# Swapped output halves for odd pairs of heads, and a first MoE block in plain float32 with its weights split later

## Chip, cores and metric

The kernel runs on one core of a Trainium2 chip. The metric is the device time of one execution in microseconds (us), and smaller is better. Four engines matter here: PE (TensorE, the matrix products; PEld is its weight loading), DVE (VectorE), ACT (ScalarE) and POOL (GpSimd). SP issues the transfers.

## The reference, cut to what matters

```python
def reference(q, k, v, f_logit, moe_w_in, moe_w_out, moe2_w_gate, moe2_w1, moe2_w2):
    f = sigmoid(f_logit)                          # 4 batches, 8 heads, 768 steps, head size 48
    for t in range(768):                          # a gated linear attention
        state = f[t][:, None] * state + k[t][:, None] * v[t][None, :]
        y[t] = q[t] @ state
    x = y as (3072 tokens, 384)
    x = relu(x @ w_in) ** 2 @ w_out               # first MoE: 384 -> 2048 -> 384
    P = sinkhorn(x @ w_gate)                      # 8 experts, 8 rounds over rows and columns
    return sum(P[:, e] * (relu(x @ w1[e]) @ w2[e]) for e in range(8))   # second MoE
```

All of it is float32. A product of two float32 matrices can be had in two ways here: as one plain float32 product, or with each operand split into a high part in the type `fp32r` and the rest (a low part), as three `fp32r` products high-high, high-low, low-high.

## The kernel before

The attention runs in 24 chunks of 128 steps (6 for each batch). For a chunk `c`, DVE makes two running products of the gates (`scan_r`, `scan_f`), POOL scales k and q with them (`mul_k`, `mul_q`), PE makes the scores (`scores`), DVE masks them (`causal`), PE turns k (`k_turn`), adds to the state (`state_in`) and mixes the outputs (`mix`), ACT and DVE take the outputs out of PSUM (`y_part`).

`mix` (lines 379 to 392) makes, for each of four pairs `p` of heads, two products "in" (L383: all 128 rows, one head to partitions 0 to 63, the other to 64 to 127) and two products "state" (L386: head j has the rows from 64 j on, and goes to the output half 64 j). The chunks that start a batch (0, 6, 12, 18) have no state. All four pairs write one PSUM tile.

Three chunks make one block of 384 tokens (8 blocks). For a block `j` the first MoE takes 16 slices `f` of the hidden layer: `e1` (`products_in`, L499) with 9 `fp32r` products (3 splits times 3 tiles of rows), then on ACT `Relu`, `Square` and the high half (`m_relu`, `m_square`, `m_hi`), on DVE the low half (`m_lo`, L515), then `e2` (`m_out`, L525) with 9 more. Slices are counted through: slice 16 is the first of block 1.

The weights of the first MoE come as 64-bit numbers, and the kernel turns them into float32 during block 0, slice by slice: `cva`, `cvw` on ACT, three DVE instructions (`clamp` L937, `fields` L941, `sign` L945), one sum on POOL (`total`, L949). Then the high half `cvh` on ACT (L280) and the low half `cvl` (L283), of which POOL makes six and DVE ten (`LO_DVE`). Block 0 waits for them slice by slice; all later blocks use the same halves.

The second MoE follows with its own weights, which go into ten buffers (`wpool`) that the first MoE's weights leave. Lines 678 and 729 are its products.

The order of the work on each engine is made by a list scheduler (`Plan`): each step has an engine, an assumed duration, a due time and the steps that it needs; of what is ready, the step with the earliest due time goes first. Engines then run their queues in that fixed order, and a waiting instruction holds up what is behind it. `keep_warm` puts dummy products (L245, plain float32, 128 columns) into PE's early gaps.

Of the kernel before, what the change touches and what calls it, by code (L numbers as in the profile page):

```python
# [20 lines left out]
NP = H // 2  # L21
# [32 lines left out]
LO_DVE = (4, 6, 8, 9, 10, 11, 12, 13, 14, 15)  # L54
# [96 lines left out]
def body(tc, fkq, v, wm, wa, wc, gate, seqs, out):  # L151
# [5 lines left out]
    wpool = ctx.enter_context(tc.tile_pool(name="wpool", bufs=NWP))  # L157
# [23 lines left out]
    wb = rpool("wb", NF - NWP)  # L181
# [82 lines left out]

    def new_w(n):
        W[n] = (wb if n >= NWP else wpool).tile([128, 2, WCOL], F32R, tag="w", name="w")
        return W[n]

    def ldw(n):
        if n in early:  # L270
            early[n] = early[n - 4] if n >= 4 else wb.tile([128, WCOL], I64, tag="w", name="raw64")
        raws[n] = early[n] if n in early else rawp.tile([128, WCOL], I64, tag="raw", name="raw64")
        sp.dma_start(out=raws[n], in_=wm[n])
# [4 lines left out]

    def cv_hi(n):
        act.copy(out=new_w(n)[:, 0, :], in_=cvt[n])  # L280

    def cv_lo(n):
        (dve if n in LO_DVE else pool).tensor_tensor(out=W[n][:, 1, :], in0=cvt[n], in1=W[n][:, 0, :].bitcast(F32), op=ALU.subtract)  # L283

    for n in range(NF):
# [3 lines left out]
        add(("cva", n), "act", 0.74, due, lambda n=n: cv_abs(n), [("ldw", n), if_(n >= 3, ("cvl", n - 3))], start=CV_AT + CV_STEP * n)  # L289
# [4 lines left out]
        add(("cvs", n), "pool", 1.78, due, lambda p=part: p("total"), [("cvb", n, 2), ("cvw", n)])  # L294
# [84 lines left out]
    def mix_pair(c, p, rows=64):  # L379
        y, vv, kk, st = tmp["y", c], vt[c % 3], kq[c % 3], Sh.get(c)  # L380
# [3 lines left out]
        if st is not None:  # L384
            for j in range(2):
                pe.matmul(y[64 * j:64 * j + rows, p, :], st[64 * j:64 * j + DH, p, 0:rows], kk[64 * j:64 * j + DH, 1, p, :], start=False, stop=True)  # L386

    def mix(c):
        new_y(c)
        for p in range(NP):  # L390
            mix_pair(c, p)
        Psb.pop(c)


    def mix_last(c):
        new_y(c)
        mix_pair(c, NP - 1)

    def last_out(c):
        act.copy(out=ylast, in_=tmp["y", c][:, NP - 1, :])  # L400

    def mix_rest(c):
        for p in range(KD):
            pe.matmul(tmp["y", c][:, p, :], shift[:, 16 * p:16 * p + 128], ylast, start=True, stop=True)
            mix_pair(c, p, DH)
# [19 lines left out]
    for c in range(NCH):  # L425
# [40 lines left out]
        needs = [("cm0", c), ("cm1", c), ("ldv", c), if_(not first, ("sh", c)), if_(1 < c < CPB, ("yl", c - 2))]  # L466
        if blk:
            at("mix", "pe", 2.1 if not first else 1.1, 2.5, mix, needs)
# [6 lines left out]
        at("yl", "dve", 0.62 if blk else 0.5, 3, lambda c: y_part(c, 1), [("yh", c)])  # L475
# [13 lines left out]
    add("conv", "none", 0, 0, close_conv, [("cvl", n) for n in range(NF)])  # L489
# [4 lines left out]
    def products_in(i, w, xx):  # L494
        ps = eps[i] = ps_e.tile([128, BT], F32, tag="e1", name="e1")
        n = 0
        for k in range(KD):
            for wl, xl in ((0, 0), (0, 1), (1, 0)):
                pe.matmul(ps, w[:, wl, k * 128:(k + 1) * 128], xx[:, xl, k, :], start=n == 0, stop=n == 3 * KD - 1)  # L499
                n += 1  # L500

    def m_relu(i):
        hl[i] = [hp.tile([128, BT], F32, tag="g", name="g", bufs=2)]
# [41 lines left out]
    E1, E2 = 1.49, 1.49  # L545
# [646 lines left out]
```

## Time and profile before

| | |
|---|---|
| median of 3 runs | 2131.81 us (2130.74 to 2133.03) |
| the profiled execution | 2132.19 us |
| its span, first to last instruction | 2130.4 us |
| busy: PE, PEld, DVE, ACT, POOL | 98%, 83%, 62%, 42%, 30% |
| mean granted TensorE clock | 0.99 |

The profile's busy shares are means over the span. The prediction reads stretches of it: a table of busy time by stretch, the list of waits of an engine, single instructions in order of time, and groups of instructions by line. In a row of instructions, "x4" counts records; a plain float32 product leaves two records of a weight load and two of a product, an `fp32r` product one of each.

### The profile page before, as it was taken

The numbers are of one execution on the slowest core, as the hardware profiler recorded it, in microseconds if no ns is written. First come the engines' busy times: TensorE is split into PE (matmuls) and PEld (weight loads), VectorE is DVE, ScalarE is ACT, GpSimd is POOL, SyncE is SP. The second block draws the span as 40 slices with busy tenths as digits, with TensorE's granted clock in tenths as the row PEclk, the third lists the DMA queues.
The fourth block names the chain that finished last, engine by engine and source line by source line (L and its number), as shares of the span: only waits on it lengthen the run. The fifth ranks groups of instructions, "written<-read, shape, count | busy, mean of one in ns | idle before, by whom it ended". The sixth has DMA issues, their size and how long they took to land.

```text
span 2130.4 us, 27837 instructions
## 1 busy us (share of the span) xinstructions
PE 2080.0 (98%) x10686; PEld 1762.8 (83%) x10686; DVE 1325.2 (62%) x2022; ACT 886.4 (42%) x1505; POOL 638.1 (30%) x636
## 2 busy tenths in 40 slices
PE   7889999999999999999999999999999999999998
PEld 5789899998987888878878888888887888888886
DVE  8973443332477666657677666756767766766674
ACT  4754444454643433423434433433433433443341
POOL 4531100010103333333332333334233243333331
PEclk9899999999999999999999999999999999999999
DMA  7342212110203111112122112121213111211210
GB/s 269 127 128 65 77 67 83 57 49 7 81 31 91 55 55 60 55 55 70 55 86 88 55 55 70 55 62 52 68 62 108 61 59 52 69 55 55 70 45 32
DMA packets 55114, 148.76 MB, mean 70 GB/s; under 512 B 6332, under 2 KB 15548, under 8 KB 54972
## 3 DMA queue, kind: packets, MB, share of 16 engines
q1 hardware_dynamic: 54972, 146.90, 21.6%
q8 instruction: 85, 1.39, 0.3%
q14 instruction: 57, 0.47, 0.1%
HBM read 135.28 MB, written 9.54 MB: 68 GB/s over the span
## 4 chain that ended last, share of the span: by engine, by line
PE 90%; DVE 6%; issue 1%; DMA 1%; POOL 1%; ACT 0%; SPq 0%; DVEq 0%; POOLq 0%; ACTq 0%
PE o L729 35%; PE e L678 33%; PE e L499 9%; PE a L525 8%; PE y L383 1%; PE y L386 1%; PE pp L344 1%; DVE cv_t L937 1%; DVE cv_t L945 1%; PE lg L540 1%; DVE lo L515 1%; PE ds L366 0%; DVE cv_t L941 0%; DVE w L283 0%; DVE sg L318 0%
## 5 line engine op out<-in xcount | busy, mean ns | idle before, releaser
L729 PE MATMUL o<-h,w 128*128 128x512 f32 x3456 | 792.8, 389 | 0.0
L729 PEld LDWEIGHTS o<-h,w 128*128 128x128 f32 x3456 | 648.1, 188 | 135.6 <-DVE sc L752 0.7
L678 PE MATMUL e<-x,w 128*128 128x512 f32 x3168 | 734.6, 391 | 10.4 <-DVE t L700 5.3
L678 PEld LDWEIGHTS e<-x,w 128*128 128x128 f32 x3168 | 597.2, 189 | 137.5 <-DVE t L700 7.0
L696 ACT COPY s<-e 128x512 f32<-128x512 f32 x288 | 168.9, 586 | 836.1 <-PE e L678 831.4
L761 POOL TENSOR_TENSOR acc<-acc,sc 128x512 f32<-128x512 f32 x258 | 334.4, 1303 | 536.4 <-DVE sc L752 529.5
L752 DVE TENSOR_TENSOR sc<-o,pb 128x512 f32<-128x512 f32 x264 | 182.0, 690 | 372.3 <-PE o L729 339.1
L718 DVE SCALAR_TENSOR_TENSOR h<-v,h 128x512 fp32r<-128x512 f32 x384 | 275.3, 736 | 1.8 <-ACT h L713 1.3
L713 ACT ACTIVATE h<-v 128x512 fp32r<-128x512 f32 x384 | 242.2, 631 | 52.8 <-DVE v L705 52.6
L705 DVE TENSOR_TENSOR v<-e,s 128x512 f32<-128x512 f32 x288 | 198.0, 688 | 74.7 <-ACT w L663 56.5
L650 POOL TENSOR_TENSOR rawa<-rawa 128x256 f32<-128x256 f32 x96 | 81.1, 845 | 537.4 <-DMA rawa<-in_wa_dram 347.8
L499 PE MATMUL e<-x,w 128*128 128x384 f32 x1152 | 229.0, 342 | 9.7 <-DVE w L283 6.2
L499 PEld LDWEIGHTS e<-x,w 128*128 128x128 f32 x1152 | 200.6, 190 | 16.7 <-DVE w L283 7.8
L515 DVE TENSOR_TENSOR lo<-g,hi 128x384 fp32r<-128x384 f32 x128 | 83.3, 653 | 208.6 <-ACT hi L511 208.6
L525 PE MATMUL a<-hi,w 128*128 128x384 f32 x768 | 200.1, 341 | 0.0
L667 DVE TENSOR_TENSOR w<-rawa,w 128x768 fp32r<-128x768 f32 x192 | 157.8, 823 | 8.1 <-ACT w L663 8.1
L663 ACT CAST w<-rawa 128x768 fp32r<-128x768 f32 x192 | 135.2, 728 | 29.6 <-DMA rawa<-in_wa_dram 12.4
L525 PE MATMUL a<-lo,w 128*128 128x384 f32 x384 | 131.0, 341 | 11.8 <-DVE lo L515 11.7
L525 PEld LDWEIGHTS a<-hi,w 128*128 128x128 f32 x768 | 140.3, 191 | 1.5 <-issue 0.3
L504 ACT ACTIVATE g<-e 128x384 f32<-128x384 f32 x128 | 62.9, 491 | 179.6 <-PE e L499 163.2
L328 POOL TENSOR_TENSOR kq<-kq,sg 128x512 f32<-128x512 f32 x24 | 30.9, 1287 | 290.7 <-DVE sg L318 161.6
L667 DVE TENSOR_TENSOR w<-rawc,w 128x768 fp32r<-128x768 f32 x96 | 92.5, 964 | 2.1 <-ACT w L663 2.0
(103 smaller groups left out, 1313.1 us busy)
## 6 DMA issues: line engine op xcount, KB each, us to landing
rawa<-in_wa_dram SPq DMA_DIRECT2D x96, 384.0 KB, 3.0
rawc<-in_wc_dram SPq DMA_DIRECT2D x96, 384.0 KB, 3.4
raw<-in_wm_dram SPq DMA_DIRECT2D x16, 768.0 KB, 6.2
pb<-ptd SPq DMA_DIRECT2D x24, 512.0 KB, 3.7
fraw<-in_fkq_dram SPq DMA_DIRECT2D x23, 512.0 KB, 4.0
kq<-in_fkq_dram SPq DMA_DIRECT2D x23, 512.0 KB, 4.6
vt<-in_v_dram SPq DMA_DIRECT2D x24, 192.0 KB, 5.0
x2d<-x2t SPq DMA_DIRECT2D x8, 576.0 KB, 2.8
```

The costliest lines, as they stand in the source:

```text
L499: pe.matmul(ps, w[:, wl, k * 128:(k + 1) * 128], xx[:, xl, k, :], start=n == 0, stop=n == 3 * KD - 1)
L525: pe.matmul(acc1[j][m], w[:, wl, D + m * 128:D + (m + 1) * 128], g, start=f == 0 and n == 0, stop=f == NF - 1 and n == 2)
L663: act.copy(out=W2[g, k][:, 0, 0:n], in_=src)
L667: dve.tensor_tensor(out=W2[g, k][:, 1, 0:n], in0=src, in1=W2[g, k][:, 0, 0:n].bitcast(F32), op=ALU.subtract)
L678: pe.matmul(ps, w[a], x[b], start=start and n == 0, stop=stop and n == 2, skip_group_check=True)
L696: act.copy(out=snap[g, n], in_=bank[g, "a"])
L705: dve.tensor_tensor(out=vs[g, k], in0=bank[g, k], in1=other, op=ALU.add)
L713: act.activation(out=hs[g // 2, t, f][:, 0], in_=vs[g, k], func=ACTF.Relu)
L718: dve.scalar_tensor_tensor(out=h[:, 1], in0=vs[g, k], scalar=0.0, in1=h[:, 0].bitcast(F32), op0=ALU.max, op1=ALU.subtract)
L729: pe.matmul(ob[q, t, m], w[:, a, c:c + 128], h[:, b], start=f == 0 and n == 0, stop=f == 3 and n == 2)
L752: dve.tensor_tensor(out=dst, in0=ob[q, t, m], in1=pbt[p, e][:, t * TB:(t + 1) * TB], op=ALU.mult)
L761: eng.tensor_tensor(out=acc[p, t, m], in0=acc[p, t, m], in1=sc[q, t, m], op=ALU.add)
```

## The change

It does four things.

1. Block 0 of the first MoE uses plain float32 products: 3 for `e1` and 3 for `e2` of a slice, straight from the converted weights `R[n]` and the unsplit `x1`, relu-square `g`. Its `m_hi`, `m_lo` and the low half of its `y_part` are gone.
2. The weights' halves are made for block 1 on: `cvh` and `cvl` are due 16 slices later, and all sixteen `cvl` are DVE's. Buffers are laid out anew: the halves of ten slices stand in `wpool`, those of six in the places of converted weights that block 0 has used.
3. The outputs of the attention go to two PSUM tiles by the parity of the pair, and in odd pairs the two heads change output halves. `mix` goes two pairs at a time: four products "in", then four "state". `y_part` takes out two pieces. The rows of `w_in` are permuted to suit.
4. The scheduler's assumed durations change (1.95 and 1.56 for a slice's products, 1.5 for `mix`), and with them the order.

```diff
-    wpool = ctx.enter_context(tc.tile_pool(name="wpool", bufs=NWP))
+    wpool = ctx.enter_context(tc.tile_pool(name="wpool", bufs=1, reuse_waits="tile"))
-    wb = rpool("wb", NF - NWP)
+    wb = rpool("wb", 1)
+    PAIR_AT = {n: n for n in range(8)} | {14: 8, 15: 9}
+    def left_by(n):
+        return [] if n in PAIR_AT else [2 * (n - 8), 2 * (n - 8) + 1]
     def new_w(n):
-        W[n] = (wb if n >= NWP else wpool).tile([128, 2, WCOL], F32R, tag="w", name="w")
-        return W[n]
+        if n in PAIR_AT:
+            t = wpool.tile([128, 2, WCOL], F32R, tag=f"w{PAIR_AT[n]}", name="w")
+            W[n] = [t[:, l, :] for l in range(2)]
+        else:
+            W[n] = [wb.tile([128, WCOL], F32R, tag=f"b{k}", name="w") for k in left_by(n)]
+    def cv_total(n):
+        R[n] = wb.tile([128, WCOL], F32, tag=f"b{n}", name="r")
+        F64(nc, cvt[n], raws[n]).total(R[n])
     def cv_lo(n):
-        (dve if n in LO_DVE else pool).tensor_tensor(out=W[n][:, 1, :], in0=cvt[n], in1=W[n][:, 0, :].bitcast(F32), op=ALU.subtract)
+        dve.tensor_tensor(out=W[n][1], in0=R[n], in1=W[n][0].bitcast(F32), op=ALU.subtract)
...
-        add(("cvh", n), "act", 0.74, due, lambda n=n: cv_hi(n), [("cvs", n), if_(n >= NF - 2, ("cvs", n - 4))])
-        add(("cvl", n), *(("dve", 0.88) if n in LO_DVE else ("pool", 1.78)), due, lambda n=n: cv_lo(n), [("cvh", n)])
+        gone = [(s, k) for k in left_by(n) for s in ("e2", "cvl")] + ([("cvs", n - 4)] if n >= 14 else [])
+        add(("cvh", n), "act", 0.8, due + NF, lambda n=n: cv_hi(n), [("cvs", n)] + gone)
+        add(("cvl", n), "dve", 0.95, due + NF, lambda n=n: cv_lo(n), [("cvh", n)])
...
     def new_y(c):
-        tmp["y", c] = (ps_p if c >= CPB else ps_acc).tile([128, NP, CH], F32, tag="pp" if c >= CPB else f"a{1 + c % 2}", name="y")
+        for n in range(2):
+            tmp["y", c, n] = (ps_p if c >= CPB else ps_acc).tile([128, NP, CH], F32, tag="pp" if c >= CPB else f"a{1 + n}", name="y")
+    def y_at(c, p):
+        return tmp["y", c, p % 2], p // 2
+    def mix_in(c, p, rows=64):
+        vv, st = vt[c % 3], Sh.get(c)
+        y, n = y_at(c, p)
         for j in range(2):
-            h = 2 * p + j
-            pe.matmul(y[64 * j:64 * j + rows, p, :], vv[:, h * DH:h * DH + rows], Psb[c][:, j, p, :], start=True, stop=st is None)
+            h, o = 2 * p + j, 64 * (j ^ (p & 1))
+            pe.matmul(y[o:o + rows, n, :], vv[:, h * DH:h * DH + rows], Psb[c][:, j, p, :], start=True, stop=st is None)
+    def mix_state(c, p, rows=64):
+        kk, st = kq[c % 3], Sh.get(c)
+        y, n = y_at(c, p)
+        for j in range(2):
+            o = 64 * (j ^ (p & 1))
+            if st is not None:
+                pe.matmul(y[o:o + rows, n, :], st[64 * j:64 * j + DH, p, 0:rows], kk[64 * j:64 * j + DH, 1, p, :], start=False, stop=True)
     def mix(c):
         new_y(c)
-        for p in range(NP):
-            mix_pair(c, p)
+        for p in range(0, NP, 2):
+            for f in (mix_in, mix_state):
+                for i in range(2):
+                    f(c, p + i)
...
     def y_part(c, lo):
-            x1[blk] = x1p.tile([128, 2, NP, BT], F32R, tag="x1", name="x1")
-        n = NP if blk else KD
-        hi, y = x1[blk][:, 0, 0:n, t0:t0 + CH], tmp["y", c][:, 0:n, :]
-        if lo:
-            dve.tensor_tensor(out=x1[blk][:, 1, 0:n, t0:t0 + CH], in0=y, in1=hi.bitcast(F32), op=ALU.subtract)
-        else:
-            act.copy(out=hi, in_=y)
+            x1[blk] = x1p.tile([128, 2, NP, BT], F32R if blk else F32, tag="x1", name="x1")
+        parts = [(slice(n, NP if blk else KD, 2), tmp["y", c, n][:, 0:2 - (n and not blk), :]) for n in range(2)]
+        for n, y in parts:
+            hi = x1[blk][:, 0, n, t0:t0 + CH]
+            if blk == 0:
+                act.copy(out=hi, in_=y)
+            elif lo:
+                dve.tensor_tensor(out=x1[blk][:, 1, n, t0:t0 + CH], in0=y, in1=hi.bitcast(F32), op=ALU.subtract)
+            else:
+                act.copy(out=hi, in_=y)
...
     def products_in(i, w, xx):
+        if i < NF:
+            for k in range(KD):
+                pe.matmul(ps, R[i][:, k * 128:(k + 1) * 128], xx[:, 0, k, :], start=k == 0, stop=k == KD - 1)
+            return
...
     def m_out(i):
         for m in range(KD):
+            if j == 0:
+                pe.matmul(acc1[j][m], R[f][:, D + m * 128:D + (m + 1) * 128], g, start=f == 0, stop=f == NF - 1)
+                continue
...
-        add(("e1", i), "pe", E1, i, lambda i=i: products_in(i, W[i % NF], x1[i // NF]),
-            [("yl", q) for q in range(CPB) if i == 0] + [if_(j == 0, ("cvl", f)), if_(f == 0 and j, ("sprd", j)), if_(i, ("e1", i - 1)), e_free(i)])
+        dur = 1.56 if j else 1.95
+        add(("e1", i), "pe", dur, i, lambda i=i: products_in(i, W.get(i % NF), x1[i // NF]),
+            [("yl", q) for q in range(CPB) if i == 0] + [if_(j == 0, ("cvs", f)), if_(j == 1, ("cvl", f)), if_(f == 0 and j, ("sprd", j)), if_(i, ("e1", i - 1)), e_free(i)])
...
-                free = ("e2", n1 - NF + n + NWP)
+                free = ("e2", n1 - NF + {v: k for k, v in PAIR_AT.items()}[n + NWP])
```

The places at which the order changes most for the prediction are two. The first is PE's queue at a mix of the attention, here that of chunk 4. L383 and L386 are "in" and "state" (L408 and L416 in the changed kernel), `pp` the scores, `a` the outputs of `e2`. Before:

```order
L366 MATMUL ds<-vt_128,Kn 64x48 x8
L383 MATMUL y<-Psb,vt_128 64x128 x2
L386 MATMUL y<-kq_122,Sh 64x128 x2
L383 MATMUL y<-Psb,vt_128 64x128 x2
L386 MATMUL y<-kq_122,Sh 64x128 x2
L383 MATMUL y<-Psb,vt_128 64x128 x2
L386 MATMUL y<-kq_122,Sh 64x128 x2
L383 MATMUL y<-Psb,vt_128 64x128 x2
L386 MATMUL y<-kq_122,Sh 64x128 x2
```

And in the changed kernel:

```order
L382 MATMUL ds<-vt_128,Kn 64x48 x8
L408 MATMUL y<-Psb,vt_128 64x128 x4
L416 MATMUL y<-kq_122,Sh 64x128 x4
L408 MATMUL y<-Psb,vt_128 64x128 x4
L416 MATMUL y<-kq_122,Sh 64x128 x4
```


Eight groups of two products became four groups of four.

The second is DVE's queue at the end of block 0, from the last conversions on. `cv_t` are the three conversion steps of a slice, `w` the low halves of the weights, `lo` the low halves of the hidden layer, `sg` and `d` belong to the scans of an attention chunk, `Psb` are masked scores. Before, from the low half of slice 13 (`lo`) on:

```order
L515 TENSOR_TENSOR lo<-g,hi 128x384
L937 TENSOR_SCALAR cv_t<-cv_t 128x768
L941 TENSOR_SCALAR cv_t<-cv_t 128x768
L945 SCALAR_TENSOR_TENSOR cv_t<-raw_1039,cv_t 128x768
L283 TENSOR_TENSOR w<-cv_t,w 128x768
L316 MEMSET sg_125 128x8
L317 MEMSET d_126 128x4
L318 SCALAR_TENSOR_TENSOR sg_125<-sg_125,d_126 128x516
L319 TENSOR_SCALAR d_126<-sg_125 128x4
L320 RECIPROCAL d_126<-d_126 128x4
L349 TENSOR_TENSOR Psb<-pp,mask 128x512
L283 TENSOR_TENSOR w<-cv_t,w 128x768
```

In the changed kernel, from the low halves of weights ahead of chunk 8's scan on (the last conversion stands ten rows further ahead):

```order
L298 TENSOR_TENSOR w<-r,w 128x768 x4
L332 MEMSET sg_124 128x8
L333 MEMSET d_126 128x4
L334 SCALAR_TENSOR_TENSOR sg_124<-sg_124,d_126 128x516
L335 TENSOR_SCALAR d_126<-sg_124 128x4
L336 RECIPROCAL d_126<-d_126 128x4
L340 SCALAR_TENSOR_TENSOR sg_124<-sg_124,d_126 128x516
L341 TENSOR_TENSOR minf<-minf,sg_124 128x4
L298 TENSOR_TENSOR w<-r,w 128x768 x5
L560 TENSOR_TENSOR lo<-g,hi 128x384
L365 TENSOR_TENSOR Psb<-pp,mask 128x512 x2
L560 TENSOR_TENSOR lo<-g,hi 128x384 x3
```

No `lo` stands among the conversions any more; the first `lo` that is left is that of slice 16, and ten low halves of weights stand between the last conversion and it (nine of them in these rows).

## Rows read from the trace of the kernel before

**Rows 1.** Busy time by stretch: us, busy (records) of each engine, PE clock, DMA, GB/s

```profile
34.08:143.65 109.57, 86.72 (x541) 74.72 (x539) 106.37 (x127) 66.68 (x108) 60.62 (x35) 0.89 0.44 142
143.65:595.60 451.95, 451.82 (x3246) 418.59 (x3246) 172.80 (x321) 223.11 (x414) 45.12 (x39) 1.00 0.19 63
```

**Rows 2.** PE's waits from 34.08 to 143.65: us in total, times, longest

```profile
PE a L525 <- DVE lo L515: 11.7, 4, 8.5
PE e L499 <- DVE w L283: 6.2, 3, 3.2
```

**Rows 3.** The chain of waits in that stretch, shares by line

```profile
by line: DVE cv_t L937 14.2%; DVE cv_t L945 13.3%; DVE lo L515 10.7%; DVE w L283 8.6%; DVE sg L318 8.4%; PE e L499 7.1%; DVE cv_t L941 7.0%; issue 6.2%; DVE sg L324 4.8%; DVE Psb L349 3.7%; DVE minf L325 3.2%; PE a L525 2.9%; DMA x<-x 2.6%;
```

**Rows 4.** In order of time: PE's and DVE's rows at slice 16's second product

```profile
140.81 0.54 DVE L515 TENSOR_TENSOR lo<-g,hi 128x384 fp32r<-128x384 f32 x1
...
142.09 1.72 PE L499 MATMUL e<-x,w 128*128 128x384 f32 x9
143.65 0.51 PE L525 MATMUL a<-hi,w 128*128 128x384 f32 x2
```

**Rows 5.** DVE and POOL in order of time: start, us, instruction

```profile
59.73 0.55 DVE L937 TENSOR_SCALAR cv_t<-cv_t 128x768 f32<-128x768 f32 x1
60.30 0.56 DVE L941 TENSOR_SCALAR cv_t<-cv_t 128x768 int32<-128x768 int32 x1
...
61.78 0.95 DVE L283 TENSOR_TENSOR w<-cv_t,w 128x768 fp32r<-128x768 f32 x1
61.99 2.44 POOL L949 TENSOR_TENSOR cv_t<-cv_t,raw 128x768 int32<-128x768 int32 x1 [2.60 <-issue]
62.65 2.20 DVE L937 TENSOR_SCALAR cv_t<-cv_t 128x768 f32<-128x768 f32 x1
...
158.28 1.23 DVE L318 TENSOR_TENSOR_SCAN sg<-sg,d 128x516 f32<-128x516 f32 x1
```

**Rows 6.** Groups by line, 34.08 to 143.65: busy us, mean ns | idle before

```profile
L937 DVE TENSOR_SCALAR cv_t<-cv_t 128x768 f32<-128x768 f32 x13 | 16.9, 1303 | 0.0
L515 DVE TENSOR_TENSOR lo<-g,hi 128x384 fp32r<-128x384 f32 x18 | 16.7, 939 | 1.0 <-ACT hi L511 1.0
...
L318 DVE TENSOR_TENSOR_SCAN sg<-sg,d 128x516 f32<-128x516 f32 x6 | 12.5, 2089 | 0.3
L283 DVE TENSOR_TENSOR w<-cv_t,w 128x768 fp32r<-128x768 f32 x10 | 11.8, 1178 | 0.0
L941 DVE TENSOR_SCALAR cv_t<-cv_t 128x768 int32<-128x768 int32 x13 | 11.2, 861 | 0.4
L324 DVE TENSOR_TENSOR_SCAN sg<-sg,d 128x516 f32<-128x516 f32 x6 | 10.3, 1709 | 0.0
...
L283 POOL TENSOR_TENSOR w<-cv_t,w 128x768 fp32r<-128x768 f32 x5 | 10.8, 2160 | 2.2 <-ACT w L280 2.2
```

**Rows 7.** The outputs of block 1: SP's issues, and the transfers' median time to landing

```profile
114.22 3.97 SPq L423 DMA_DIRECT2D x<-x  x6
...
x<-x SPq DMA_DIRECT2D x6, 48.0 KB, 6.0
```

**Rows 8.** PE in order of time: dummy products in plain float32, and what follows

```profile
37.54 2.62 PE L245 MATMUL warm<-shift 128*128 128x128 f32 x22
39.91 3.65 PE L499 MATMUL e<-x,w 128*128 128x384 f32 x18
```

**Rows 9.** PE in order of time: products of mixes (chunks 7, 6 and 5)

```profile
164.16 0.40 PE L383 MATMUL y<-Psb,vt 128*64 128x128 f32 x4
164.49 0.44 PE L386 MATMUL y<-kq,Sh 48*64 48x128 f32 x4
164.86 0.44 PE L383 MATMUL y<-Psb,vt 128*64 128x128 f32 x4
...
167.06 1.83 PE L499 MATMUL e<-x,w 128*128 128x384 f32 x9
...
150.87 1.09 PE L383 MATMUL y<-Psb,vt 128*64 128x128 f32 x16
...
105.60 0.43 PE L383 MATMUL y<-Psb,vt 128*64 128x128 f32 x2
```

**Rows 10.** DVE: the outputs of chunk 7 leave PSUM

```profile
167.93 0.66 DVE L415 TENSOR_TENSOR x<-y,x 128x512 fp32r<-128x512 f32 x1
```

More of the change, by code (lines that the diff above doesn't have):

```diff
@@ L277, in cv_abs @@
         F64(nc, cvt[n], raws[n]).magnitude()
+    def cv_total(n):
+        R[n] = wb.tile([128, WCOL], F32, tag=f"b{n}", name="r")
+        F64(nc, cvt[n], raws[n]).total(R[n])
     def cv_hi(n):
-        act.copy(out=new_w(n)[:, 0, :], in_=cvt[n])
+        new_w(n)
+        act.copy(out=W[n][0], in_=R[n])
     def cv_lo(n):
-        (dve if n in LO_DVE else pool).tensor_tensor(out=W[n][:, 1, :], in0=cvt[n], in1=W[n][:, 0, :].bitcast(F32), op=ALU.subtract)
+        dve.tensor_tensor(out=W[n][1], in0=R[n], in1=W[n][0].bitcast(F32), op=ALU.subtract)
     for n in range(NF):
@@ L396, in mix_last @@
         new_y(c)
-        mix_pair(c, NP - 1)
+        mix_in(c, NP - 1)
+        mix_state(c, NP - 1)
     def last_out(c):
-        act.copy(out=ylast, in_=tmp["y", c][:, NP - 1, :])
+        act.copy(out=ylast, in_=tmp["y", c, 1][:, 1, :])
     def mix_rest(c):
         for p in range(KD):
-            pe.matmul(tmp["y", c][:, p, :], shift[:, 16 * p:16 * p + 128], ylast, start=True, stop=True)
-            mix_pair(c, p, DH)
+            y, n = y_at(c, p)
+            pe.matmul(y[:, n, :], shift[:, 16 * p:16 * p + 128], ylast, start=True, stop=True)
+            mix_in(c, p, DH)
+            mix_state(c, p, DH)
         Psb.pop(c)
@@ L465, in body @@
             at("sh", "dve", 0.35, 0, shat, [("st", c - 1), ("scanr", c), if_(c % NCB > 2, ("mix", c - 2))])
-        needs = [("cm0", c), ("cm1", c), ("ldv", c), if_(not first, ("sh", c)), if_(1 < c < CPB, ("yl", c - 2))]
+        needs = [("cm0", c), ("cm1", c), ("ldv", c), if_(not first, ("sh", c)), if_(0 < c < CPB, ("yl", c - 1))]
         if blk:
-            at("mix", "pe", 2.1 if not first else 1.1, 2.5, mix, needs)
+            at("mix", "pe", 1.5 if not first else 0.95, 2.5, mix, needs)
         else:
@@ L487, in close_conv @@
         pools["x2t"] = rpool("x2p", 2)
-    add("conv", "none", 0, 0, close_conv, [("cvl", n) for n in range(NF)])
+    add("conv", "none", 0, 0, close_conv, [("cvs", n) for n in range(NF)])
     hl, x2t, x2, eps = {}, {}, {}, {}
@@ L496, in products_in @@
         n = 0
+        if i < NF:
+            for k in range(KD):
+                pe.matmul(ps, R[i][:, k * 128:(k + 1) * 128], xx[:, 0, k, :], start=k == 0, stop=k == KD - 1)
+            return
         for k in range(KD):
             for wl, xl in ((0, 0), (0, 1), (1, 0)):
-                pe.matmul(ps, w[:, wl, k * 128:(k + 1) * 128], xx[:, xl, k, :], start=n == 0, stop=n == 3 * KD - 1)
+                pe.matmul(ps, w[wl][:, k * 128:(k + 1) * 128], xx[:, xl, k, :], start=n == 0, stop=n == 3 * KD - 1)
                 n += 1
     def m_relu(i):
-        hl[i] = [hp.tile([128, BT], F32, tag="g", name="g", bufs=2)]
+        hl[i] = [hp.tile([128, BT], F32, tag="hi", name="g") if i < NF else hp.tile([128, BT], F32, tag="g", name="g", bufs=2)]
         act.activation(out=hl[i][0], in_=eps.pop(i), func=ACTF.Relu)
@@ L518, in m_out @@
         j, f = divmod(i, NF)
-        _, hi, lo = hl.pop(i)
-        w = W[f]
+        g, *parts = hl.pop(i)
         if f == 0:
@@ L523, in m_out @@
         for m in range(KD):
+            if j == 0:
+                pe.matmul(acc1[j][m], R[f][:, D + m * 128:D + (m + 1) * 128], g, start=f == 0, stop=f == NF - 1)
+                continue
+            hi, lo = parts
             for n, (wl, g) in enumerate(((0, hi), (1, hi), (0, lo))):
-                pe.matmul(acc1[j][m], w[:, wl, D + m * 128:D + (m + 1) * 128], g, start=f == 0 and n == 0, stop=f == NF - 1 and n == 2)
+                pe.matmul(acc1[j][m], W[f][wl][:, D + m * 128:D + (m + 1) * 128], g, start=f == 0 and n == 0, stop=f == NF - 1 and n == 2)
         if j == NB - 1:
@@ L543, in logits_out @@
         dve.tensor_copy(out=L[:, CPB * j:CPB * (j + 1), :], in_=tmp["l"])
-    E1, E2 = 1.49, 1.49
     def e_free(i):
@@ L660, in w2_hi @@
     def w2_hi(g, k):
-        W2[g, k] = wpool.tile([128, 2, WCOL], F32R, tag="w", name="w2")
+        W2[g, k] = wpool.tile([128, 2, WCOL], F32R, tag=f"w{(3 * g + 'abc'.index(k)) % NWP}", name="w2")
         src, n = w2src(g, k)
@@ L945, in sign, with total @@
         dve.scalar_tensor_tensor(out=ti, in0=self.high, scalar=-0x40000000, in1=ti, op0=ALU.bitwise_and, op1=ALU.bitwise_or)
-    def total(self):
+    def total(self, out=None):
         ti = self.t.bitcast(I32)
-        self.nc.gpsimd.tensor_tensor(out=ti, in0=ti, in1=self.word.bitcast(I32), op=ALU.add)
+        self.nc.gpsimd.tensor_tensor(out=ti if out is None else out.bitcast(I32), in0=ti, in1=self.word.bitcast(I32), op=ALU.add)
     def all(self):
@@ L1160, in lay_out @@
     for kt in range(KD):
-        rows += [2 * kt * DH + r for r in range(DH)]
-        rows += [6 * DH + 16 * kt + r for r in range(16)]
-        rows += [(2 * kt + 1) * DH + r for r in range(DH)]
-        rows += [7 * DH + 16 * kt + r for r in range(16)]
+        for j in range(2):
+            rows += [(2 * kt + (j ^ (kt & 1))) * DH + r for r in range(DH)]
+            rows += [(7 - j) * DH + 16 * kt + r for r in range(16)]
     w_in = inputs["moe_w_in"][np.array(rows)]
```

36 lines of the change are left out of this document (19 added, 17 removed).

## Prediction

> **What bounds the kernel now.** I read the table of busy time by stretch first, because the change touches two stretches that have different limits. From 34 us, when block 0's products begin, to 143.65 us, when the second products of slice 16 begin, DVE is busy for 106.4 of 109.6 us and PE for 86.7; from there to the end of the first MoE PE is busy for 451.8 of 451.95 us [rows 1]. So in block 0 DVE sets the pace, and behind it PE alone. The other views say the same: PE waits in block 0 mostly for DVE's low halves of the hidden layer (11.7 us in 4 waits) and of the weights (6.2 us in 3) [rows 2], and the chain of waits runs through DVE's conversions, low halves and scans [rows 3]. What is taken from DVE in block 0, or from PE after it, should come off the end one for one.
>
> I compare the kernels at one point: the start of slice 16's second product, 143.65 us before [rows 4]. By then either order has PE done with the same steps: first products to slice 18, second ones to slice 15, attention to the scores of chunk 6.
>
> **Part 1, block 0 on DVE.** DVE's queue up to slice 16's low half, which begins at 140.81 us [rows 4], loses 16 low halves of the hidden layer, 0.55 us each undisturbed [rows 4] (8.8), three low halves of block 0's outputs (about as long, 1.65), and the masking of chunk 6's scores, which now stands behind it (1.3). It gains the six weight halves that POOL made, 0.95 us each undisturbed [rows 5] (5.7), and three takings-out in two pieces for one (0.5 in all, if half of 0.66 [rows 10] costs 0.4). Neighbours on DVE overlap by some 0.1 us, which takes 1 from the difference. That leaves 5 us.
>
> More comes from POOL. A DVE instruction that meets a POOL instruction waits for it: the clamp takes 0.55 us alone, and 2.20 us where POOL's sum of 2.44 us has just begun [rows 5]. Against undisturbed durations of 0.55, 0.55, 1.23, 0.95, 0.56 and (taken as the other scan's) 1.23 [rows 4, 5], the six DVE groups shown are longer by 9.8, 7.0, 5.2, 2.3, 3.9 and 2.9 us [rows 6], 31 us together, while POOL is busy for 60.6 [rows 1]. So a us of POOL costs DVE about 0.51. The halves that leave POOL are five of 2.16 us here [rows 6] and one more before the stretch, 13 us: 6.6 us less waiting. The sixteen sums stay.
>
> Slice 16's low half then begins at 140.8 - 5 - 6.6 = 129.2 and ends at 129.8, and its product follows at about 129.9 us: **13.8 us earlier**. Before, PE reached that point last; now DVE does, because the deferred weight halves do not vanish: ten of them stand between the last conversion and that low half. I end nothing sooner than this queue allows.
>
> *What the plain float32 products cost PE.* 22 records of the dummy product, eleven products of 128 columns, take 39.91 - 37.54 = 2.37 us [rows 8], 0.215 us each. For 384 columns that is 0.65 us, 1.94 for a slice's three, against 143.65 - 142.09 = 1.56 us for nine `fp32r` ones [rows 4]. 32 times 0.38 are 12.2 us more PE work, costed at nothing: PE idles for 22.9 us in this stretch [rows 1]. Without waits PE needs, from 34 us, 32 x 1.94, three first products of block 1 (4.7) and attention work of about 14 us, so it could be there at 115 us. Were that cover gone, the 12.2 us would be on the path.
>
> *Queues passed.* Block 1's outputs are taken out behind the last conversion (at about 108 us by the same reckoning). Their six transfers take 4.0 us to issue and 6.0 us to land [rows 7], so slice 16's first product starts by 118 us; 9.7 us of PE work from there lead to 128 us, just under 129.9. On SP a load of the second MoE now stands ahead of them; the sum it waits for is done by then. ACT loses 16 casts in block 0 and is busy for 66.7 of 109.6 us [rows 1]; costed at nothing. Two of the ten weight buffers come free for the second MoE at the last two slices of the first; they hold parts that are used over 30 us later; nothing.
>
> **Part 2, the mixes behind block 0.** Fifteen chunks with a state (7 to 11, 13 to 17, 19 to 23) have their mix where PE is the bound. One takes 167.06 - 164.16 = 2.90 us [rows 9]: eight groups of two products, one each 0.37 us (164.49 to 164.86). Two things in the rows matter. A group of one product (2 records) takes 0.43 us, as long as a group of two (0.44) that stand in different parts of the array [rows 9]: they run side by side. And eight pairs-in-a-row products of one kind, 16 records, take 1.09 us where the first pair takes 0.44: 0.217 for each further pair, not 0.37 [rows 9]. So 0.15 us per group is start and finish between kinds.
>
> A group of four "in" uses two column halves twice: 0.37 + 0.217 = 0.585 us. A group of four "state" has four different quarters (row half and column half), because of the swapped halves; if all run side by side it takes 0.37 us. A mix is then 2 x (0.585 + 0.37) = 1.91 us, 1.0 less, fifteen times: **15 us**. No row shows four quarters at work, so this price has bounds. Below: no gain at all, if every change of partner costs a start and finish as now; nearer, four quarters two by two, 2 x 1.17 = 2.34 us, a gain of 0.56 and 8.4 us in all. Above: the four starts and finishes hidden too, about 1.3 us, a gain of 1.6 and 24 us. I take 15, since the rows with one and two parts show no cost for the second. Chunks 6, 12, 18 have no state and stay as they are; those of block 0 lie under DVE.
>
> A rule of the Trainium skill speaks against it. The rows first: a "state" group (L386) puts the two row halves into one PSUM tile, and its four records take the same 0.44 us as an "in" group [rows 9]. The Trainium skill, "TensorEngine Tiling", section "Restrictions and Gotchas" (PSUM Pressure), says that different row tiles cannot access the same PSUM bank simultaneously. The trace does not agree where the column halves differ, so I give it little weight; by it a state group would go two by two, the 2.34 us above, and the sum would be 6.6 us more.
>
> **The sum.** 2132.2 - 13.8 - 15.0 = 2103.4 us, against the profiled execution, which lies 0.4 us above the median of the runs. A measurement can tell about 0.2%, 4.3 us, from no change.
>
> **The rivals.**
> - *Quarters two by two.* Only half of the state products overlap further: 2132.2 - 13.8 - 8.4 = 2110 us. For it: no row has four parts; against: two cost as one. Chance 0.2.
> - *DVE gets less.* The weight halves are moved, not removed, and meet POOL's sums on DVE as the low halves did (0.51 us a us); if the lighter POOL only shifts its sums into other DVE instructions, part 1 is the 5 us alone, or a little more: 2132.2 - 6 - 15 = 2111 us. Chance 0.16.
> - *More from either.* Starts and finishes partly hidden, or DVE's end at 125 us: about 2094 us. Chance 0.12.
> - *Slower: scores wait for outputs.* Both buffers that the scores use are now the outputs' too, so a chunk's scores wait until ACT and DVE have emptied them. Now that takes from 167.06 to 168.59 us [rows 9, 10]; in two pieces about 2 us. PE's order puts at least one slice (3.1 us) between, which covers it. If a scan (3 us of DVE) slips in ahead each time, it is 5 us, a wait of 1.9 for some twenty chunks, 38 us: 2141 us. It decides against the change from 1.4 us a chunk on. Against: DVE's order has the taking-out first nearly everywhere. Chance 0.05.
>
> **How the numbers follow.** The forecast has 0.47. Its own range, 2098 to 2108, is widened to the first three rivals: 2092 to 2115, which leaves out the slower one and the outer bounds. Faster by over 0.2% are all cases but the slower one and a sliver of the second and third added up (no gain from mixes and little from DVE): 0.92; the sliver 0.03; slower 0.05.
>
> **What would show it.** In the changed profile PE's waits in block 0 should be about 10 to 15 us, with the largest before slice 16's second product or at conversions; slice 16's second product should start near 130 us; a slice's plain products should take 1.94 us; a mix in the later blocks 1.9 us in four groups of 0.585 and 0.37, and PE should stay without waits from there on. A state group of 0.585 us would show the first rival; a start of slice 16's product past 136 us the second; waits of the scores for `x` (the outputs) the last. The prediction is wrong if PE waits for something new behind block 0, or if DVE's queue is not what holds slice 16's product.

## The result, and the profile after

| | before | changed |
|---|---|---|
| median of 4 runs | 2132.42 us | 2109.32 us (2106.10 to 2111.75) |
| the profiled execution | 2132.19 us | 2111.75 us |
| its span | 2130.4 us | 2110.0 us |

The ratio is 0.9892, with a 95% interval of 0.9874 to 0.9909: the kernel is faster by 23.1 us. 2103.4 was forecast; the time lies in the range of 2092 to 2115, and the gain is 80% of the one forecast (28.8). The profiled execution is the highest of the four.

The table of busy time by stretch, changed kernel, cut at the same points as [rows 1] (slice 16's second product; the end of the first MoE's last logits); columns as there:

```profile
34.08:135.88 101.80, 89.89 (x432) 54.16 (x429) 96.83 (x120) 60.40 (x97) 50.29 (x30) 0.93 0.46 156
135.88:572.67 436.79, 436.66 (x3246) 413.48 (x3246) 178.41 (x339) 223.49 (x432) 47.52 (x39) 1.00 0.20 65
572.67:2110.00 1537.33, 1510.25 (x6638) 1244.62 (x6637) 1019.77 (x1529) 581.19 (x958) 520.33 (x542) 1.00 0.19 61
```

The two terms of the sum can be read off here.

| | before | changed | difference | forecast |
|---|---|---|---|---|
| slice 16's second product starts | 143.65 | 135.88 | -7.8 | -13.8 |
| from there to the end of the first MoE | 451.95 | 436.79 | -15.2 | -15.0 |
| the second MoE (to the end of the span) | 1534.8 | 1537.3 | +2.5 | 0 |

The third line's 2.5 us can't be told from scatter. In the profiles of the ten runs below the second MoE lasted 1533.4 to 1538.9 us; the same changed kernel had 1537.3 in one profile and 1535.1 in another. So a difference of less than some 5 us there says nothing about a kernel. I read the other two lines. The first line scatters too: in the changed kernel's other profile slice 16's second product starts at 134.84 us (more of this in part 1 of the experiments).

**The mix.** PE in order of time, changed kernel: chunk 7's mix and the product behind it.

```profile
156.38 0.62 PE L408 MATMUL y<-Psb,vt 128*64 128x128 f32 x8
156.94 0.45 PE L416 MATMUL y<-kq,Sh 48*64 48x128 f32 x8
157.32 0.66 PE L408 MATMUL y<-Psb,vt 128*64 128x128 f32 x8
157.90 0.45 PE L416 MATMUL y<-kq,Sh 48*64 48x128 f32 x8
158.28 1.83 PE L544 MATMUL e<-x,w 128*128 128x384 f32 x9
```

From start to next start, the "in" groups take 0.56 and 0.58 us, the "state" groups 0.38: four products in four quarters take as long as two did [rows 9]. A mix takes 158.28 - 156.38 = 1.90 us for 2.90; fifteen of them are 15.0 us.

**Block 0.** First the list of PE's waits in the changed kernel from 34 to 140 us (us in total, times, longest), then PE, ACT and DVE in order of time near its end.

```profile
PE e L540 <- ACT g L549: 6.2, 3, 3.3
PE pp L360 <- DVE x L453: 2.6, 1, 2.6
PE y L408 <- DVE Psb L365: 2.1, 1, 2.1
```

```profile
107.52 2.17 PE L540 MATMUL e<-x,r 128*128 128x384 f32 x6 [1.56 <-ACT g L549]
...
112.97 2.17 PE L540 MATMUL e<-x,r 128*128 128x384 f32 x6 [1.34 <-ACT g L549]
114.98 2.10 PE L569 MATMUL a<-g,r 128*128 128x384 f32 x6
120.35 3.21 PE L540 MATMUL e<-x,r 128*128 128x384 f32 x6 [3.28 <-ACT g L549]
123.36 2.79 PE L569 MATMUL a<-g,r 128*128 128x384 f32 x6
125.70 2.03 PE L544 MATMUL e<-x,w 128*128 128x384 f32 x9
...
135.88 0.51 PE L573 MATMUL a<-hi,w 128*128 128x384 f32 x2
```

```profile
118.99 0.83 ACT L295 CAST w<-r 128x768 fp32r<-128x768 f32 x1 [4.89 <-DVE w L298]
119.73 0.48 ACT L549 ACTIVATE g<-e 128x384 f32<-128x384 f32 x1
```

```profile
116.16 5.33 DVE L298 TENSOR_TENSOR w<-r,w 128x768 fp32r<-128x768 f32 x4
...
130.62 0.55 DVE L560 TENSOR_TENSOR lo<-g,hi 128x384 fp32r<-128x384 f32 x1
```

PE's waits for low halves of the hidden layer and of the weights [rows 2] are gone. What is left is 11.9 us of idle time (101.80 - 89.89), but the largest item is new: plain products of `e1` (L540) that wait for ACT's relu (L549). The third wait, at 120.35, is for the relu of slice 13, which frees the PSUM buffer for slice 15. That relu could have run sooner: the product it reads, slice 13's first, began at 107.52 us. It stood in ACT's queue behind the high half of slice 12's weights (L295), which goes into places that converted weights leave, and so had waited 4.89 us for DVE's low halves made from those weights. PE then starts slice 15 at 120.35, and works through to 135.88 without a pause. DVE had slice 16's low half ready at 131.2.

The clock adds to it. The stretches around that wait, changed kernel (columns as above; the granted clock is the last but two):

```profile
112.97:117.10 4.13, 4.11 (x12) 2.16 (x12) 4.03 (x7) 1.13 (x2) 1.93 (x2) 1.00 0.49 108
117.10:120.35 3.25, 0.00 (x0) 0.03 (x1) 3.25 (x4) 1.33 (x3) 3.17 (x3) 1.00 0.13 49
120.35:124.35 4.00, 4.00 (x8) 2.33 (x9) 3.77 (x8) 2.88 (x6) 2.56 (x3) 0.62 0.00 0
```

Behind the idle 3.25 us the granted clock is 0.62 on average over 4 us (0.5 is the level of 1.2 GHz, 1.0 that of 2.4 GHz), and the two groups of plain products take 3.21 and 2.79 us for 2.10: 1.8 us are lost.

### The profile page after: what moved, and what is told of

Its sections match the earlier page's. It is cut to its first block, busy times and chain, and to the rows that moved or that the text cites. A ratio compares the mean times of both kernels' runs of the same rounds, so it can differ in the third digit from the quotient of the medians.

```text
span 2110.0 us, 27581 instructions
## 1 busy us (share of the span) xinstructions
PE 2065.1 (98%) x10558; PEld 1734.0 (82%) x10558; DVE 1318.5 (62%) x2030; ACT 880.3 (42%) x1513; POOL 629.2 (30%) x630
## 4 chain that ended last, share of the span: by engine, by line
PE 90%; DVE 6%; issue 1%; DMA 1%; POOL 1%; ACT 0%; SPq 0%; DVEq 0%; POOLq 0%; ACTq 0%
PE o L780 35%; PE e L729 32%; PE e L544 9%; PE a L573 8%; PE pp L360 1%; PE y L408 1%; PE lg L588 1%; DVE cv_t L996 1%; DVE cv_t L992 1%; DVE cv_t L988 1%; PE y L416 1%; DMA rawa<-in_wa_dram 1%; DVE w L298 1%; PE ds L382 0%; DVE sg L334 0%
## 5 line engine op out<-in xcount | busy, mean ns | idle before, releaser
L729 PEld LDWEIGHTS e<-x,w 128*128 128x128 f32 x3168 | 596.2, 189 | 138.3 <-ACT s L747 8.0
L544 PE MATMUL e<-x,w 128*128 128x384 f32 x1008 | 198.1, 339 | 0.0
L560 DVE TENSOR_TENSOR lo<-g,hi 128x384 fp32r<-128x384 f32 x112 | 67.9, 606 | 201.1 <-ACT hi L556 200.5
L544 PEld LDWEIGHTS e<-x,w 128*128 128x128 f32 x1008 | 173.9, 188 | 4.8 <-issue 2.4
L573 PE MATMUL a<-hi,w 128*128 128x384 f32 x672 | 171.9, 336 | 0.0
L549 ACT ACTIVATE g<-e 128x384 f32<-128x384 f32 x128 | 62.8, 491 | 160.8 <-PE e L544 148.8
L573 PEld LDWEIGHTS a<-hi,w 128*128 128x128 f32 x672 | 120.6, 188 | 0.9
L573 PE MATMUL a<-lo,w 128*128 128x384 f32 x336 | 112.4, 335 | 0.0
```

Source lines behind the costliest of these rows:

```text
L544: pe.matmul(ps, w[wl][:, k * 128:(k + 1) * 128], xx[:, xl, k, :], start=n == 0, stop=n == 3 * KD - 1)
L573: pe.matmul(acc1[j][m], W[f][wl][:, D + m * 128:D + (m + 1) * 128], g, start=f == 0 and n == 0, stop=f == NF - 1 and n == 2)
L729: pe.matmul(ps, w[a], x[b], start=start and n == 0, stop=stop and n == 2, skip_group_check=True)
```

## Experiments

All times are medians, the kernel before between 2131.1 and 2132.7 in each set. "Slice 16" is short for the start of slice 16's second product in the profile, "the rest" for the time from there to the end of the first MoE.

### Part 2: what in the mix gives the 15 us

**One pair at a time** (one_pair_at_a_time), with swap and both PSUM tiles kept:

```diff
-        for p in range(0, NP, 2):
+        for p in range(NP):
             for f in (mix_in, mix_state):
-                for i in range(2):
+                for i in range(1):
                     f(c, p + i)
```

> The changed kernel, but the mix goes one pair at a time again (two 'in', two 'state'); swap and two PSUM tiles stay. Theory A (each change between 'in' and 'state' costs about 0.15 us, and four changes are saved, with the partner products hidden): eight groups of 0.37 us, a mix of 2.9 us, time 15 us above the changed kernel, that is about 2124. Rival B (two PSUM tiles or the swap let neighbouring groups overlap even so): a mix of 2.4 us or less, time up by under 8 us.

Measured: 2124.78 us, 15.5 above the changed kernel. PE, that kernel, chunk 7's mix (the first two of eight groups, the last, and the product behind):

```profile
159.82 0.40 PE L408 MATMUL y<-Psb,vt 128*64 128x128 f32 x4
160.16 0.44 PE L416 MATMUL y<-kq,Sh 48*64 48x128 f32 x4
...
162.36 0.44 PE L416 MATMUL y<-kq,Sh 48*64 48x128 f32 x4
162.73 1.83 PE L544 MATMUL e<-x,w 128*128 128x384 f32 x9
```

The mix is back at 2.91 us, and the rest at 451.90 against 451.95 before. Theory A holds; the swap and the two tiles alone give nothing. This run is also part 1 by itself, with the new tiles: 7.8 us below before.

**Not swapped** (not_swapped), with the grouping kept (and the rows of `w_in` to match):

```diff
-            h, o = 2 * p + j, 64 * (j ^ (p & 1))
+            h, o = 2 * p + j, 64 * j
...
-            o = 64 * (j ^ (p & 1))
+            o = 64 * j
```

> The changed kernel, but in odd pairs the two heads keep their output halves as in the kernel before (the rows of w_in to match); the order four 'in', four 'state' and the two PSUM tiles stay. Theory A (the swap puts the four state products into four different quarters, which run side by side): without it two and two share a quarter, so a state group takes as long as an 'in' group, 0.59 us from start to next start instead of 0.37; a mix takes 2.36 us instead of 1.93, and the time rises by 15 x 0.44 = 6.5 us. Rival B (grouping alone gives the gain): a state group stays at 0.37 us, and the time stays within 2 us.

Measured: 2115.60 us, 6.3 above the changed kernel. PE, that kernel, chunk 7's mix:

```profile
155.99 0.62 PE L408 MATMUL y<-Psb,vt 128*64 128x128 f32 x8
156.55 0.65 PE L416 MATMUL y<-kq,Sh 48*64 48x128 f32 x8
157.13 0.66 PE L408 MATMUL y<-Psb,vt 128*64 128x128 f32 x8
157.72 0.65 PE L416 MATMUL y<-kq,Sh 48*64 48x128 f32 x8
158.30 1.83 PE L544 MATMUL e<-x,w 128*128 128x384 f32 x9
```

A state group takes 0.58 us, a mix 2.31, the rest 442.92 (6.1 more). Theory A again. So of the 15 us some 9 come from fewer changes between "in" and "state", and 6 from the swap, which lets the four state products run side by side. Two pairs at a time without it is what the first rival of the prediction priced (2.34).

**The mix alone** (mix_alone) on the kernel before: the change's new functions of the outputs (`new_y` to `y_part`), the rows of `w_in` and `mix`'s assumed duration; block 0 is left as it was.

```diff
-        for p in range(NP):
-            mix_pair(c, p)
+        for p in range(0, NP, 2):
+            for f in (mix_in, mix_state):
+                for i in range(2):
+                    f(c, p + i)
```

> The kernel before with the new mix alone: swap, two PSUM tiles, two pairs at a time, outputs taken out in two pieces; block 0 stays as it was, in three fp32r products with halves made in time. Theory A (the two parts of the change add up): slice 16's second product stays at 143 to 145 us, the stretch from there to the last logits of the first MoE is 15 us shorter than the 451.97 us before, and the time is about 2117. Rival B (part of the gain behind block 0 comes from the weights' new places or the new order, not from the mix): the stretch is shorter by 11 us or less. Rival C (the smaller pieces of the outputs cost block 0 more than 2 us on DVE, which the deferred halves hid in the changed kernel): slice 16's second product at 146 us or later.

Measured: 2119.54 us, 13.0 below before; the rest is 436.01. Slice 16 is at 146.61, but a mix of 0.92 us (chunk 6's, which has no state) now stands ahead of it. Without that, the rest is 15.0 us shorter, and slice 16 is 2 us later, at 145.7: between the 145 of theory A and the 146 of rival C. Of these 2 us, 0.7 are there when block 0's products begin (34.83 us for 34.08). PE's list of waits in block 0 (that kernel, 30 to 150 us) has

```profile
PE a L545 <- DVE lo L535: 20.8, 5, 8.5
```

where [rows 2] has 11.7. So A holds for the gain. That block 0 loses something agrees with the median, 13.0 us below before where the mixes alone give 15.0; whether the smaller pieces of the outputs (rival C) or the new order cost it was not separated.

### Part 1: what held the end of block 0

One thing has to be taken out of the starts of slice 16 first: block 0's first product begins at another time in each execution, 32.9 to 38.7 us in the profiles of the changed kernel and its variants. Counted from there, in us (two numbers are two profiles of the same kernel):

| | block 0's first product | slice 16's second product | between |
|---|---|---|---|
| before | 34.08 | 143.65 | 109.57 |
| changed kernel | 35.23, 34.24 | 135.88, 134.84 | 100.65, 100.60 |
| halves_after_relu | 36.42, 34.61 | 131.91, 132.92 | 95.49, 98.31 |
| halves_after_conversions | 33.02, 35.66 | 126.53, 129.17 | 93.51, 93.51 |
| halves_at_once | 34.19 | 139.19 | 105.00 |
| six_low_halves_on_pool | 32.85 | 140.13 | 107.28 |

The two edits to the changed kernel's mix leave this length as it is (100.65 in one_pair_at_a_time, 100.68 in not_swapped). So block 0 itself became 8.9 us shorter by the change.

**High halves behind the last relu** (halves_after_relu). Those of slices 8 to 13 only:

```diff
-        add(("cvh", n), ..., [("cvs", n)] + gone)
+        add(("cvh", n), ..., [("cvs", n)] + gone + ([("r", NF - 1)] if left_by(n) else []))
```

> The changed kernel, but the high halves of the weights of slices 8 to 13 are made only after the last relu of block 0. Theory A (in the changed kernel the end of block 0 is held by ACT: a high half that waits for DVE's low halves stands ahead of the relu of slice 13, 118.99 us after a wait of 4.9, and the products behind it then run at a lower clock): with the relus free, the first product of slice 15 starts near 115 us instead of 120.35, slice 16's second product at 128 to 130 us instead of 135.88, and the time falls by 6 to 8 us, to about 2102. Rival B (DVE's queue alone holds that point, as the prediction had it): ACT's wait goes, but slice 16's second product starts no earlier than its low half allows, 130.6 us less what the moved low halves free; if the moved halves only shift DVE's waits for POOL, 134 us or later, and the time falls by less than 2 us.

Measured: 2103.37 us (2102.75 to 2107.33), and slice 16 at 131.91; the rest 436.80, as in the changed kernel. PE is the later of the two there by 2 us: slice 16's low half was ready at 129.9. That is 4.0 us sooner at the point, and 5.2 counted from block 0's first product, less than A's 6 to 8; a wait of 1.6 us for a relu stayed. PE, that kernel:

```profile
110.23 2.17 PE L540 MATMUL e<-x,r 128*128 128x384 f32 x6 [1.59 <-ACT g L549]
```

The kernel was run again in a later set, with the changed kernel beside it:

> The kernel of halves_after_relu once more. Theory A of that run: 5 to 7 us below the changed kernel. If the 6 us there were a matter of that one set of runs: less than 3 us.

> The changed kernel once more, beside the two that follow, to tell differences of some us: 2106 to 2112.

Measured: 2109.15 us, and 2109.30 for the changed kernel. The gain in time is not shown. The traces say why: slice 16 was at 132.92 against 134.84, and block 0 took 98.31 us where it took 95.49 in the first run. Here PE and ACT of this second run:

```profile
108.38 4.18 PE L540 MATMUL e<-x,r 128*128 128x384 f32 x6 [3.01 <-ACT g L549]
112.35 3.09 PE L569 MATMUL a<-g,r 128*128 128x384 f32 x6
```

```profile
107.02 0.83 ACT L295 CAST w<-r 128x768 fp32r<-128x768 f32 x1 [1.35 <-POOL r L1000]
107.75 0.48 ACT L549 ACTIVATE g<-e 128x384 f32<-128x384 f32 x1
```

The edit left the high halves of slices 14 and 15 ahead of relus, and one of them waits 1.35 us for POOL's sum of its slice. A wait of the same kind is left: PE stood for 3 us, and the granted clock behind it was 0.51 for 6 us.

**All high halves of slices 8 to 15 behind the last relu, all low halves behind the last conversion** (halves_after_conversions).

```diff
-        add(("cvh", n), ..., [("cvs", n)] + gone)
-        add(("cvl", n), ..., [("cvh", n)])
+        add(("cvh", n), ..., [("cvs", n)] + gone + ([("r", NF - 1)] if n >= 8 else []))
+        add(("cvl", n), ..., [("cvh", n), ("cvb", NF - 1, 2)])
```

> The changed kernel, but all deferred low halves wait for the last conversion, and the high halves of slices 8 to 15 for the last relu of block 0. Theory A (what still holds block 0 with ACT's relus free is the conversions, among which six deferred low halves stand on DVE): the last conversion ends about 7 us sooner than the 110.75 us of halves_after_relu, PE's 1.6 us wait for a relu goes and its other waits shrink, slice 16's second product starts at 126 to 129 us instead of 131.91, and the time is 2098 to 2101. Rival B (PE is the bound of block 0 by now, or the outputs of block 1 come no sooner): the conversions end sooner, but slice 16's second product starts at 130 us or later and the time stays at 2102 to 2105. Rival C (the low halves, now all late, hold up the first products of block 1): PE waits for a low half of a weight before slices 17 to 20, and the time rises.

> The kernel of halves_after_conversions once more. Its slice 16 had its second product 5.4 us sooner than that of halves_after_relu, and its second MoE lasted 5.5 us longer in the profiled execution. Theory A (that length varies from execution to execution, 1533 to 1539 us in the profiles so far, with no tie to the kernel): it comes out 3 to 6 us below after_relu_again. Rival B (the second MoE starts no earlier for another reason, so that what is won in block 0 is given back): within 2 us of it, and the second MoE is again 3 us or more longer in the profile.

Measured: 2102.54 us, and in the later set 2101.91 (2100.86 to 2102.83) beside the changed kernel's 2109.30 (2108.09 to 2110.46): 7.4 us less, with no overlap. Slice 16 was at 126.53 and 129.17, in both profiles 93.51 us behind block 0's first product. PE's stretch from slice 12's first product to there, first run:

```profile
100.61:126.53 25.92, 25.73 (x104) 16.77 (x102) 25.71 (x29) 15.82 (x29) 12.20 (x8) 1.00 0.26 77
```

PE is busy for 25.73 of 25.92 us at full clock, with no wait for a relu at all. In the changed kernel the same stretch (101.93 to 135.88) takes 33.95 us, 8.0 more: 6.2 of waits for relus and 1.8 of the clock. The second run has 25.94 us here. But one expectation fell: the last conversion ended at 109.5, and at 112.1 in the second run, no sooner than in the changed kernel (109.6 and 108.6); A had it 7 us sooner than the 110.8 of halves_after_relu. With the low halves away, the scheduler put two scans ahead of it. So it is ACT's queue that gave the time, not the conversions. The second MoE lasted 1538.9 and 1534.2 us in the two profiles of this one kernel, which bears out that this length has no tie to the change. It is the fastest of the kernels run.

**Halves at once** (halves_at_once), due as in the kernel before:

```diff
-        add(("cvh", n), "act", 0.8, due + NF, ...)
-        add(("cvl", n), "dve", 0.95, due + NF, ...)
+        add(("cvh", n), "act", 0.8, due, ...)
+        add(("cvl", n), "dve", 0.95, due, ...)
```

> The changed kernel with the halves of the weights due as in the kernel before, so that DVE makes twelve low halves ahead of the last conversion instead of six (those in left places must still wait for their places). Theory A (what part 1 gave is the low halves of the hidden layer that left DVE and the six that left POOL; the deferral only moves work within DVE's queue): the last conversion ends some 6 to 8 us later, near 117 us, but nothing is left behind it, and slice 16's second product starts at 133 to 138 us, the time within 3 us of the changed kernel. Rival B (the deferral is what gives the gain): slice 16's second product starts at 141 us or later and the time is 5 to 8 us longer, about 2116.

Measured: 2113.42 us (2108.99 to 2115.04), 4.1 above the changed kernel of that set; slice 16 at 139.19. It lies between the two theories. The last conversion ended at 121.2, and the one before it had PE wait 4.8 us for POOL's sum:

```profile
119.28 4.21 PE L540 MATMUL e<-x,r 128*128 128x384 f32 x6 [4.83 <-POOL r L1000]
```

So the deferral does more than A had it, about 4 us (4.4 counted from block 0's first product).

**Six low halves on POOL again** (six_low_halves_on_pool), on top of halves_after_relu:

```diff
+LO_POOL = (0, 1, 2, 3, 5, 7)
...
-        dve.tensor_tensor(out=W[n][1], in0=R[n], ...)
+        (pool if n in LO_POOL else dve).tensor_tensor(out=W[n][1], in0=R[n], ...)
...
-        add(("cvl", n), "dve", 0.95, due + NF, ...)
+        add(("cvl", n), *(("pool", 1.9) if n in LO_POOL else ("dve", 0.95)), due + NF, ...)
```

> The kernel of halves_after_relu, but six low halves of weights (slices 0, 1, 2, 3, 5, 7) are POOL's again, as in the kernel before. Theory A (a us of POOL costs DVE 0.5 us of waiting, so that moving the six from POOL to DVE changed little): DVE loses 6 x 0.95 = 5.7 us of its own work and gains about 6.5 us of waiting; slice 16's low half starts within 2 us of the 129.35 us there, and the time stays within 2 us of 2103.4. Rival B (POOL's work does not hold DVE up much): slice 16's low half starts 4 to 6 us sooner, near 124 us, and the last conversion with it.

Measured: 2116.68 us. The last conversion ended at 118.7 instead of 110.8, slice 16's low half began at 133.64. The stretch up to the last `sign` of halves_after_relu, then of this kernel:

```profile
34.08:109.88 75.80, 67.36 (x350) 39.58 (x348) 73.71 (x90) 47.34 (x74) 40.98 (x22) 0.93 0.58 198
```

```profile
34.08:117.70 83.62, 66.94 (x327) 39.63 (x326) 81.83 (x94) 45.36 (x70) 54.78 (x29) 0.89 0.47 173
```

Rival B falls: DVE's last conversion didn't come sooner but 8 us later. Theory A's 2 us fall too: the time is 13 us longer than in the first run of halves_after_relu, 7.5 than in the second. The order differs too (two low halves instead of six ahead of the point, but two first scans and one second scan more), so I add up all of DVE's instructions there, each at the shortest length of its group: 53.7 and 53.1 us. DVE was busy for 73.71 and 81.83. POOL's 13.8 us more cost DVE 8.8 us: 0.64 a us, not 0.5, from one pair of profiles. PE's scores then waited 10.4 us for outputs that DVE took out late (`pp` for `x`), the mechanism of the prediction's slower rival, called up by another cause; so the time is no measure of POOL's share alone.

A mix with all eight "in" ahead of all eight "state" would save two more changes. It would hold two open sums in one PSUM tile, and was not tried.

## Why the prediction was right, and where it was off

That the time lies in the range is in part luck. It is outside the forecast's own 2098 to 2108; the range was widened by three rivals, none of whose mechanisms the changed kernel shows. And the prediction's last sign of being wrong came true: DVE's queue is not what held slice 16's product.

- **Which engine bounds which stretch.** Right. Behind block 0 PE has no waits (436.66 of 436.79 us), and what a mix lost came off the end one for one: undoing the grouping put the same 15 us back.
- **Part 2.** Right in size and reason: a mix of 1.91 us was forecast and 1.90 measured, and the stretch lost 15.2 us for 15.0. The three prices taken from [rows 9] (0.37 for the first pair in a group, 0.217 for a further one on the same parts, none for one on other parts) carried over to four quarters, which no row had shown. The rival "quarters two by two" describes the unswapped kernel instead. The PSUM Pressure rule of the Trainium skill, "TensorEngine Tiling (Array Packing)", section "Restrictions and Gotchas", says that different row tiles cannot access the same PSUM bank at the same time. The trace doesn't agree: a state group takes 0.38 us, though both row halves write each of its two PSUM tiles.
- **Part 1, DVE's queue.** Nearly right: slice 16's low half began at 130.62 us, where 129.2 was worked out, and block 0's products began 1.2 us later than before. The groups by line of the changed kernel, 34.08 to 135.88 us (busy us, mean ns | idle before), answer to [rows 6]:

```profile
L298 DVE TENSOR_TENSOR w<-r,w 128x768 fp32r<-128x768 f32 x16 | 21.5, 1383 | 0.0
L996 DVE SCALAR_TENSOR_TENSOR cv_t<-raw,cv_t 128x768 int32<-128x768 int32 x14 | 14.3, 1021 | 0.5
L988 DVE TENSOR_SCALAR cv_t<-cv_t 128x768 f32<-128x768 f32 x13 | 13.3, 1026 | 0.0
L992 DVE TENSOR_SCALAR cv_t<-cv_t 128x768 int32<-128x768 int32 x14 | 12.6, 901 | 0.4
...
L334 DVE TENSOR_TENSOR_SCAN sg<-sg,d 128x516 f32<-128x516 f32 x6 | 10.9, 1816 | 0.4
L340 DVE TENSOR_TENSOR_SCAN sg<-sg,d 128x516 f32<-128x516 f32 x6 | 10.4, 1734 | 0.2
```

  Against undisturbed times (0.95, 0.96, 0.55, 0.56, 1.23, 1.23) they are longer by 6.9, 0.9, 6.2, 4.8, 3.5 and 3.0 us, 25 us together for POOL's 50.29: 0.50 a us, as assumed. That counts the large groups alone; what POOL's extra work cost over all of DVE's instructions, in the run with halves on POOL, was 0.64.
- **Plain products.** Right: a slice's three were forecast at 1.94 us and take 1.93 (from 92.06 to the next start at 93.99 in the changed kernel), and PE still idled for 11.9 us, in the 10 to 15 named. The cover was thinner than worked out, though: PE was busy for 89.9 us of the stretch where the prediction's working gives 81 (34 to 115 us), as products also ran at a lower clock (at 56.98 us a slice's three took 3.64 us, at a granted clock of 0.60).
- **The term that was mis-sized** is part 1's 13.8 us, which measured 7.8, and the step that failed is "ACT loses 16 casts in block 0 and is busy for 66.7 of 109.6 us [rows 1]; costed at nothing". A busy share says nothing about order. The deferred high halves stand in ACT's queue among the relus that PE waits for, and they wait for low halves on DVE, which take longer than the scheduler assumes (1.38 us in the mean for 0.95). So PE came to slice 15 at 120.35, and from there needed 15.5 us, 1.8 of them lost to the lower clock. "Now DVE does" (reach the point last) was wrong by this: DVE was done at 131.2, 1.3 us behind the 129.9 forecast, and PE 4.7 us after that: the 6.0 us that are missing. With ACT's relus free of those high halves (halves_after_conversions) block 0 was 7.1 us shorter, and the time 7.4. The prediction asked, for each queue, how full it is; of ACT's it did not ask what the new instructions there wait for.
- **The rival "DVE gets less"** has the time (2111), but not the mechanism: it put the loss on POOL's sums in DVE instructions, and named a start past 136 us as its mark; the start was at 135.88, and held by PE's wait for ACT.
- **The slower rival** is seen in block 0 alone, where scores wait for outputs once: 2.6 us in this profile, 5.5 in the changed kernel's other one. Behind block 0 there is none.

## What to carry to other kernels

Work that is deferred doesn't only leave a queue, it goes to another place in it: read what stands behind it there and what it waits for, on each engine, before costing it at nothing. An in-order engine at 60% busy can still hold up the chain if one instruction in it waits for a slower engine. For small matrix products that use a part of the array, put products of one kind side by side on different row and column parts, and change kinds seldom: here the rows of two parts gave the price of four to 0.01 us a mix.

## What was not expected of the hardware

- A wait of PE costs more than its length where the clock falls behind it: 3.25 us idle were followed by 4 us at a granted clock of 0.62 (1.8 us lost), and in after_relu_again 3.0 us idle by 6 us at 0.51 (4.18 and 3.09 us for 2.10 each, 3.1 us lost). In the two runs of halves_after_conversions, without such waits, the granted clock was 1.00 from slice 12's first product to slice 16's second.
- A us of POOL's elementwise work cost DVE 0.5 to 0.64 us by these estimates, and handing 0.95 us DVE instructions to POOL, where they took 2.4 us each (six_low_halves_on_pool), made DVE later, not sooner.
